# A gated mix of local attention and a GeGLU FFN: two down weights' low parts on VectorE in the second FFN, and one operand group copied two places later

## Chip, core and metric

The kernel runs on one core of one Trainium2 chip. The metric is the device time of one execution in microseconds; the median of three runs is compared. A core has five engines that work side by side, each through its own instructions in a fixed order: TensorE (PE, with PEld for loading its weights), VectorE (DVE), ScalarE (ACT), GpSimd (POOL) and SyncE (SP, which here issues most DMAs). They wait for one another through semaphores. On-chip memory is SBUF; matmul results go to PSUM, in banks of 128 x 512 floats.

## What is computed

```python
x = A_x                                                # 2048 tokens x 512
g = _sigmoid((x * gate_w).sum(-1, keepdims=True))
a = _A_ref(x, A_wqkv, A_wo)                            # 32 heads of 16; each token sees 8 tokens, 2 apart
b = (_gelu(x @ w_gate) * (x @ w_up)) @ w_down          # 512 -> 1792 -> 512
return g * a + (1 - g) * b
```

In `_A_ref` queries, keys and values come from `x @ wqkv`; each query takes a softmax over the 8 keys at distances 0, 2, ..., 14 and mixes those values; the result goes through `wo`. All inputs are float32.

## The kernel before

**Two halves.** The tokens are split into even and odd ones (`par` 0 and 1), since attention at distance 2 never mixes the two. The order is: queries, keys, values of half 0; FFN of half 0 (`ffn(0)`, here the first FFN); the same for half 1 (`ffn(1)`, the second FFN); then the last products of attention with `wo`. Attention itself (scores, softmax, mix) is VectorE work on 128 x 2048 tiles. It is written as one long generator, `attention()`, and `pull(budget)` takes about so many microseconds of it at many points of the program, so that it runs beside TensorE's products.

**Two parts of every operand.** To keep float32 precision on TensorE, every operand is split into a high part (the value rounded to the matmul's type, `float32r`) and a low part (value minus high part), and each product is three matmuls: high x high, high x low, low x high. A low part is made in one of two ways:

- on VectorE: ScalarE copies the value to the high part, then VectorE subtracts it (`tensor_tensor`, lines 725 and 762);
- by DMA: ScalarE writes the negated high part where the low part is to be, then POOL issues a DMA that adds the value to it in memory (lines 732 and 765), and ScalarE writes the high part later (lines 734 and 767).

**The FFN.** It runs over 14 chunks of 128 hidden columns (`f`, `FC = 14`). In a chunk, gate and up are computed together as one 2 x 2 block product in seven block products instead of eight (a Strassen-Winograd form: `a11`, `a12`, `s1` ... on the token side, `b11`, `t1`, ... on the weight side). `gate_up` (line 833) writes them in this order: a11 x b11, s1 x t1, the a22 x t4 of the chunk before (`fourth`), s2 x t2, a12 x b21, s4 x b22, s3 x t3. Each is six matmuls of line 774. ScalarE empties the banks (lines 779, 785, 851, 866, 882), VectorE adds (786), multiplies gate by up (790) and, after ScalarE's high part (792), makes the low part of the hidden rows (793).

Between the products there are nine **places**, `idle(0)` to `idle(8)`. At place i the steps that `ffn` registered with `at(i, ...)` are put, and a budget of attention is pulled. There are also four **pieces**: in chunks 0 and 1 of the first FFN the last projections (`project_one`), in chunks 0 and 1 of the second the last two key products (`key_one`, line 512, whose results POOL adds to memory in lines 509 and 510), and from chunk 2 on the down products of an earlier pair of chunks (`down`, line 805, matmuls in line 816). One down product takes 128 tokens through both chunks of a pair: three matmuls with the first chunk's hidden rows and down weights, three with the second's. So chunk 2's pieces, the first down products, need the down weights and the hidden rows of chunks 0 and 1.

**What a chunk prepares for the next.** In chunk f, `ffn` registers for chunk f + 1:

- `operands(par, f + 1, 0)`, the first group (t1, t2, b11), two steps. In the first FFN the first step is the ScalarE copy of line 721 and the second VectorE's subtraction of line 725; the parts are then stored in memory (`keep_parts`, at place 0 of the next chunk). In the second FFN the first step is one DMA issue on SP's queue that reads those stored parts back (line 715, 768 KB), and the second does nothing.
- `operands(par, f + 1, 1)`, the second group, made by DMA (729, 732 and 734).
- `fetch_d`, the load of raw down weights (695), and `down_w`, which splits them. Chunks 0 and 1 have theirs split together, in chunk 1, at places 3 and 7.

**What sets the order.** The text of the kernel gives the order in which instructions are traced. A planner in the compiler then orders each engine's instructions by priority (the traced order, with attention put 150 places behind by `pull`) on a timeline of its own, and assigns buffers: a tile is given a buffer of its tag when an earlier one is free (`g0`, the first groups, has two; `d`, the down weights, four). An instruction wrapped in `paced` isn't planned before the last matmul traced ahead of it. On the chip each engine goes through the planned order and waits where data isn't there.

The constants that matter: `WARM`, `BEHIND = 150`, `PACE = (0.9, 1.22)`, and `BUFS` in line 52.

Of the kernel before, what the change touches and what calls it, by code (L numbers as in the profile page):

```python
# [44 lines left out]
def tile_gated_mix(ctx: ExitStack, tc: tile.TileContext, xt, wqkv, wff, wo, out):  # L45
# [11 lines left out]
    def tl(tag, dt=F32):  # L57
        return pool.tile([P, COLS.get(tag, 512)], dt, name=tag, bufs=BUFS[tag])
# [453 lines left out]
    def key_one(k, t):  # L512

        if k == 5:
            KB[t] = bank(f"acc{t}")
        key_mm(KB[t], t, *KEYS[k], (0, 1), k == 5)
        st = tl("rt")
        nc.scalar.activation(st, KB[t], AF.Copy)
        store_b(nc.gpsimd, st, BT + t if k == 5 else t, 1, accum_op=OP.add)
        pull(1.1)  # L520
        if k == 6 and t == BT - 1:
            done.add((1, 2))

    def project_one(par, jj):

        ps = bank(f"acc{jj % BT}")
        qkv_mm(ps, par, jj, 2, range(KC))
        take(ps, par, jj, 1, tag=None if jj < 5 else "c")
        pull((2.7, 2.2)[par])
        if jj == NP - 1:  # L530
            done.add((par, 2))
# [94 lines left out]
    def paced(ins):  # L626

        tc.add_manual_dep(ins.ins, LAST[-1].ins.name, mybir.DependencyInfo(mybir.DependencyClass.Sync,
                          mybir.DependencyReason.SCHED_ONLY), reason="pace")
# [76 lines left out]
    def operands(par, f, i):  # L706


        n = len(GROUPS[i]) * QW
        w = tl(f"g{i}", F32R)  # L710
        hi, lo = w[:, :n], w[:, n:2 * n]
        for k, op in enumerate(GROUPS[i]):
            WG[f, op] = hi[:, k * QW:(k + 1) * QW], lo[:, k * QW:(k + 1) * QW]
        if par and not i:
            nc.sync.dma_start(w[:, :2 * n].bitcast(F32), WS[f, i])
            yield
            return
        raw = RAW[f][:, (0, 4)[i] * QW:][:, :n]
        if not i:
            KEEP[f] = w[:, :2 * n]  # L720
            ins = nc.scalar.activation(hi, raw, AF.Copy)
            if f:
                paced(ins)
            yield
            ins = nc.vector.tensor_tensor(lo, raw, hi.bitcast(F32), op=OP.subtract)
            if f:
                paced(ins)
            return
        ins = nc.scalar.activation(lo, raw, AF.Copy, scale=-1.0)  # L729
        if par and not f:  # L730
            paced(ins)
        nc.gpsimd.dma_start(lo.bitcast(F32), raw, accum_op=OP.add)  # L732
        yield
        ins = nc.scalar.activation(hi, raw, AF.Copy)
        if par or f:
            paced(ins)

    def keep(f):

        WS[f, 1] = dram.tile([P, 2 * QW], F32, name=f"ws{f}1")  # L740
        paced(nc.sync.dma_start(WS[f, 1], RAW[f][:, 5 * QW:7 * QW]))
# [13 lines left out]
    def down_w(par, f):  # L755
        d = WD[f] = tl("d", F32R)
        rd = RD.pop(f)
        if not par and f < 2:

            paced(nc.scalar.activation(d[:, :512], rd, AF.Copy))  # L760
            yield
            paced(nc.vector.tensor_tensor(d[:, 512:], rd, d[:, :512].bitcast(F32), op=OP.subtract))
            return
        paced(nc.scalar.activation(d[:, 512:], rd, AF.Copy, scale=-1.0))  # L764
        nc.gpsimd.dma_start(d[:, 512:].bitcast(F32), rd, accum_op=OP.add)  # L765
        yield
        paced(nc.scalar.activation(d[:, :512], rd, AF.Copy))
# [37 lines left out]
    def down(par, gr, t, b):  # L805
        if b == t == gr == 0:
            ACC.update((t, bank(f"acc{t}")) for t in range(BT))
        pp = bank("p") if b else ACC[t]
        if b and gr:
            nc.scalar.activation(pp, RT[BT + t], AF.Copy)  # L810
        ts = slice(t * P, (t + 1) * P)
        for i in range(2):
            hh_, hl_ = Hs[2 * gr + i, b]
            d = WD[2 * gr + i]
            for n, (a, w) in enumerate(((hh_, d[:, :512]), (hh_, d[:, 512:]), (hl_, d[:, :512]))):
                LAST[:] = [nc.tensor.matmul(pp, a[:, ts], w, start=(i == 0 and n == 0 and gr == 0),  # L816
                                            stop=(i == 1 and n == 2), skip_group_check=True)]
        jj = BT * b + t
        if gr == NG - 1 and par:
            nc.scalar.activation(pp, pp, AF.Copy, scale=gc[:, par, jj:jj + 1])  # L820
            ACC[jj] = pp
        elif gr == NG - 1:
            st = tl(("s", "c")[t % 2])[:, :512]
            nc.scalar.activation(st, pp, AF.Copy, scale=gc[:, par, jj:jj + 1])
            nc.gpsimd.dma_start(out_v[2 * jj], st)
        elif b:
            if gr == 0:
                RT[BT + t] = tl("rt")
            nc.scalar.activation(RT[BT + t], pp, AF.Copy)
        if par or gr < NG - 2:  # L830
            pull(1.2 * PACE[par])
# [95 lines left out]
    def ffn(par):  # L927
        XOP.update(((n, kc), X[par, blk, kc + k]) for n, blk, k in (("a11", 0, 0), ("a12", 0, 2), ("a22", 1, 2))
                   for kc in range(2))
        todo = iter(())  # L930
        for f in range(FC):
            do = {}

            def at(i, x, *args):
                do.setdefault(i, []).append(lambda: x(*args))

            if par and f < 2:
                pieces = [[lambda t=t: key_one(5 + f, t)] for t in range(BT)]
            elif f > 1:
                pieces = [[lambda b=b, i=i: down(par, f // 2 - 1, f % 2 * 2 + i, b)] for b in range(2) for i in range(2)]  # L940
            else:
                pieces = [[lambda jj=jj: project_one(par, jj) for jj in jjs]
                          for jjs in (((0, 1), (2, 3), (4, 5), (6,)), ((7,), (), (), ()))[f]]
            if f + 1 < FC:
                for i in range(2):
                    steps = operands(par, f + 1, i)
                    at(1 + 2 * i, next, steps, None)
                    at(5 + i, next, steps, None)
                at(0 if f != 1 else 5, fetch_d, f + 1)
                for g_ in ((), (0, 1))[f] if f < 2 else (f,):  # L950
                    steps = down_w(par, g_)
                    at(2 if f > 2 else 4 - f % 2, next, steps, None)
                    at(7, next, steps, None)
            else:
                steps = down_w(par, f)
                at(1, next, steps, None)
                at(4, next, steps, None)
            if par:
                if f + 2 < FC:
                    at(0, fetch_sums, f + 2)  # L960
                else:
                    at(0, fetch_o) if f + 2 == FC else None
                if f + 1 == FC:
                    todo = chain(load_o(), channels_of(0, 0))
                    for i in range(1, 9):
                        at(i, next, todo, None)
            else:
                if f + 2 < FC:
                    at(1, fetch, f + 2)
                    at(8, combine, f + 2)  # L970
                else:
                    at(0, fetch_x, 1, f + 2 - FC)
                if f + 1 < FC:
                    do.setdefault(0, []).insert(0, lambda: keep(f + 1))
                at(0, keep_parts, f)
                if f + 2 == FC:
                    at(8, early)
                if f + 1 == FC:
                    todo = before()
                    for i in range(2, 9):  # L980
                        at(i, next, todo, None)
            gate_up(par, f, pieces, do)
        for _ in todo:
            pass
        fourth()
        if par:
            out_first()
            oT = {}
        ends = iter(()) if par else tail()
        for b in range(2):  # L990
            for t in range(BT):
                down(par, NG - 1, t, b)
                if par and t == 0:
                    oT[0, b] = channels(par, 0, b)
                next(ends, None)
        if par:
            finish(oT)
# [10 lines left out]
    def load_o():  # L1008
        t = tl("g1", F32R)
        cols = [t[:, i * 512:(i + 1) * 512] for i in range(4)]  # L1010
        for u in range(NU):
            raw = WO[u]
            WO[u] = hi, lo = pair("S") if u > 1 else cols[2 * u:2 * u + 2]
            split_by_dma(hi, lo, raw)
            yield
# [213 lines left out]
```

## Time and profile before

| | us |
|---|---|
| median of three runs (606.63 to 607.61) | 606.99 |
| the profiled execution | 607.57 |
| its span, first to last instruction | 605.8 |
| PE busy in the span | 593.1 |
| DVE busy | 534.1 |
| ACT busy | 415.0 |
| POOL busy | 93.2 |

The mean granted clock of TensorE in the profiled execution is 0.994 of full speed.

How to read the rows: a row of the order of time is start, duration, engine, line, operation, output<-inputs by the names of tiles, shapes, and the number of instructions merged; in square brackets is how long the engine sat idle before it and for what. A row of the waits table is engine, line and tile that waited, what ended the wait, then total us, how often, and the longest. A row of stretches is the stretch, its length, busy time with instruction count of PE, PEld, DVE, ACT and POOL, then the granted clock, the share of DMA engines busy and GB/s. In rows of the chain of waits an entry `DMA d<-r` is the time from the issue of a DMA to its landing. SPq marks what SP's queue does.

### The profile page before, as it was taken

The page shows a single profiled execution, that of the slowest core. Times are in us where ns is not written, and L with a number is a line of the kernel's source. Part 1 is how long each engine was busy: PE and PEld are TensorE (multiplying, and loading weights), DVE is VectorE, ACT ScalarE, POOL GpSimd, SP SyncE. Part 2 cuts the span into 40 slices and gives each one's busy share as a digit, 9 for nine tenths or more (in the row PEclk, how much of TensorE's full clock was granted, in tenths as well). Part 3 has the DMA queues.
Part 4 walks back from the last instruction along what each step waited for, and adds up shares of the span by engine and source line. Part 5 has one row for each costly group of instructions (what it writes and reads, how often), then busy time and mean ns, then how long its engine had stood idle before and what let it go on. Part 6 is the DMA issues. An engine that isn't in the chain of part 4 may idle for free.

```text
span 605.8 us, 8237 instructions
## 1 busy us (share of the span) xinstructions
PE 593.1 (98%) x2767; PEld 495.8 (82%) x2767; DVE 534.1 (88%) x626; ACT 415.0 (68%) x724; POOL 93.2 (15%) x116
## 2 busy tenths in 40 slices
PE   9999989999999999999999997999999999999997
PEld 7898868888888888888899876888888888888885
DVE  6958899997999979997989993999799989998981
ACT  6663666678776787778876673766776687696622
POOL 0140000111111111112001671111111111121300
PEclk9999999999999999999999997999999999999999
DMA  8795996959786886998999999588967896967824
GB/s 281 248 265 163 288 310 200 272 159 277 193 211 210 239 239 187 246 293 254 271 273 324 268 270 289 153 215 207 259 174 184 233 253 165 240 161 200 118 63 156
DMA packets 90808, 136.47 MB, mean 225 GB/s; under 512 B 8463, under 2 KB 54671, under 8 KB 90766
## 3 DMA queue, kind: packets, MB, share of 16 engines
q1 hardware_dynamic: 70542, 102.98, 52.6%
q0 software_dynamic: 15584, 30.48, 27.4%
q10 hardware_dynamic: 4640, 2.49, 1.4%
q8 instruction: 21, 0.34, 0.2%
q14 instruction: 21, 0.17, 0.1%
HBM read 69.83 MB, written 42.56 MB: 186 GB/s over the span
## 4 chain that ended last, share of the span: by engine, by line
PE 87%; DMA 7%; ACT 1%; DVE 1%; SPq 1%; issue 1%; ACTq 0%; DVEq 0%
PE p L774 40%; PE acc L816 13%; PE p L816 13%; PE p L1046 5%; PE acc L504 5%; PE acc L406 2%; DMA d<-r 2%; PE p L355 2%; PE p L406 2%; PE acc L355 2%; PE acc L1046 2%; DMA kq<-kq 1%; DMA qs<-hl 1%; PE p L504 1%; DMA qs<-c 1%; DMA vs<-hl 1%
## 5 line engine op out<-in xcount | busy, mean ns | idle before, releaser
L774 PE MATMUL p<-S,g 128*128 128x512 f32 x672 | 168.6, 390 | 0.7 <-ACT s L779 0.7
L774 PEld LDWEIGHTS p<-S,g 128*128 128x128 f32 x672 | 126.3, 188 | 27.3 <-ACT s L779 1.1
L774 PE MATMUL p<-A,g 128*128 128x512 f32 x504 | 125.3, 389 | 1.0 <-ACT c L882 1.0
L774 PEld LDWEIGHTS p<-A,g 128*128 128x128 f32 x504 | 94.4, 188 | 20.8 <-ACT c L882 1.4
L567 DVE TENSOR_TENSOR prod<-kq 128x2048 f32<-128x2048 f32 x32 | 72.9, 2278 | 4.6 <-DMA kq<-kq 4.4
L605 DVE TENSOR_TENSOR prod<-v,lg 128x2048 f32<-128x2048 f32 x32 | 72.9, 2279 | 0.9
L570 DVE TENSOR_REDUCE lg<-prod 128x128 f32<-128x2048 f32 x32 | 73.0, 2282 | 0.2
L816 PE MATMUL p<-d,hh 128*128 128x512 f32 x224 | 68.6, 389 | 0.0
L816 PE MATMUL acc<-d,hh 128*128 128x512 f32 x224 | 60.5, 395 | 4.6 <-DMA d<-r 4.6
L732 POOL DMA_DIRECT2D g<-raw x28 | 24.3, 868 | 230.5 <-ACT g L729 133.1
L785 ACT ACTIVATE c<-p 128x512 f32<-128x512 f32 x56 | 33.4, 597 | 32.6 <-PE p L774 32.6
L816 PEld LDWEIGHTS acc<-d,hh 128*128 128x128 f32 x224 | 42.7, 191 | 13.9 <-DMA d<-r 5.0
L779 ACT ACTIVATE s<-p 128x512 f32<-128x512 f32 x56 | 33.1, 594 | 23.6 <-PE p L774 22.8
L816 PEld LDWEIGHTS p<-d,hh 128*128 128x128 f32 x224 | 42.0, 188 | 8.7
L793 DVE TENSOR_TENSOR hl<-c,hh 128x512 fp32r<-128x512 f32 x56 | 38.3, 684 | 11.2 <-ACT hh L792 11.1
L765 POOL DMA_DIRECT2D d<-r x26 | 22.3, 858 | 159.7 <-ACT d L764 133.5
L816 PE MATMUL p<-d,hl 128*128 128x512 f32 x112 | 42.6, 389 | 0.0
L786 DVE TENSOR_TENSOR c<-c,s 128x512 f32<-128x512 f32 x56 | 38.3, 684 | 3.4 <-ACT c L785 3.1
L792 ACT ACTIVATE hh<-c 128x512 fp32r<-128x512 f32 x56 | 35.1, 627 | 7.6 <-DVE c L790 7.3
L609 DVE TENSOR_TENSOR prod<-prod 128x1024 f32<-128x1024 f32 x32 | 39.0, 1219 | 0.2
L790 DVE TENSOR_TENSOR c<-c 128x512 f32<-128x512 f32 x56 | 38.2, 684 | 0.5 <-ACT c L882 0.2
L816 PE MATMUL acc<-d,hl 128*128 128x512 f32 x112 | 36.0, 395 | 0.0
(213 smaller groups left out, 993.6 us busy)
## 6 DMA issues: line engine op xcount, KB each, us to landing
g<-raw POOLq DMA_DIRECT2D x28, 512.0 KB, 7.2
raw<-wff SPq DMA_DIRECT2D x42, 256.0 KB, 3.9
ws<-g SPq DMA_DIRECT2D x14, 768.0 KB, 5.6
g<-ws SPq DMA_DIRECT2D x14, 768.0 KB, 7.6
r<-wff SPq DMA_DIRECT2D x28, 256.0 KB, 4.1
d<-r POOLq DMA_DIRECT2D x26, 256.0 KB, 6.7
v<-vs SPq DMA_DIRECT2D x8, 512.0 KB, 6.3
os<-tb SPq DMA_DIRECT2D x64, 64.0 KB, 4.7
```

Source lines behind the costliest of these rows:

```text
L504: LAST[:] = [nc.tensor.matmul(ps, x[:, ts], w, start=(start and kc == i == 0), stop=(kc == 1 and i == 2), skip_group_check=True)]
L567: paced(nc.vector.tensor_tensor(prod, spans(k, jj), q[:, jj:jj + 2, None, :].to_broadcast([P, 2, W, UC]), op=OP.mult))
L570: nc.vector.tensor_reduce(two_of(lg, jj), prod.rearrange("p j w (h d) -> p (j w) h d", d=DH), axis=AX.X, op=OP.add)
L605: paced(nc.vector.tensor_tensor(prod.rearrange("p j w (h d) -> p (j w) h d", d=DH), spans(v, jj).rearrange("p j w (h d) -> p j w h d", d=D ...
L609: nc.vector.tensor_tensor(prod[:, :, :4], prod[:, :, :4], prod[:, :, 4:], op=OP.add)
L774: LAST[:] = [nc.tensor.matmul(ps, w_, a_, start=(start and kc == 0 and n == 0), stop=(kc == 1 and n == 2), skip_group_check=True)]
L786: nc.vector.tensor_tensor(c, c, s, op=OP.add)
L790: nc.vector.tensor_tensor(ge, ge, up, op=OP.mult)
L792: nc.scalar.activation(hh_, ge, AF.Copy)
L793: nc.vector.tensor_tensor(hl_, ge, hh_.bitcast(F32), op=OP.subtract)
L816: LAST[:] = [nc.tensor.matmul(pp, a[:, ts], w, start=(i == 0 and n == 0 and gr == 0), stop=(i == 1 and n == 2), skip_group_check=True)]
L1046: LAST[:] = [nc.tensor.matmul(pa, a, b, start=(first and n == 0), stop=(last and n == 2), skip_group_check=True)]
```

## The change

```diff
@@ -755,7 +755,7 @@
     def down_w(par, f):
         d = WD[f] = tl("d", F32R)
         rd = RD.pop(f)
-        if not par and f < 2:
+        if f < 2:
 
             paced(nc.scalar.activation(d[:, :512], rd, AF.Copy))
             yield
@@ -944,7 +944,7 @@
             if f + 1 < FC:
                 for i in range(2):
                     steps = operands(par, f + 1, i)
-                    at(1 + 2 * i, next, steps, None)
+                    at(1 + 2 * (i or f == 1), next, steps, None)
                     at(5 + i, next, steps, None)
                 at(0 if f != 1 else 5, fetch_d, f + 1)
                 for g_ in ((), (0, 1))[f] if f < 2 else (f,):
```

The first edit concerns the second FFN alone (`par` = 1): the low parts of the down weights of chunks 0 and 1 are made by VectorE, as in the first FFN, and no longer by DMA. At place 3 of chunk 1 ScalarE then writes the high parts, at place 7 VectorE subtracts. Lines 764, 765 and 767 keep the other 24 down weights.

The second edit concerns chunk 1 of both FFNs: the first step for chunk 2's first group stands at place 3 instead of place 1. At place 3 it is traced ahead of the second group's first step and of the first steps of `down_w`. In all other chunks the expression gives the same places as before.

## The prediction

> **What bounds the kernel now.** I read the page first: its engine table, then the table of who waited for whom on TensorE, then the order of time around the one long wait.
>
> ```profile
> span 605.8 us, 8237 instructions
> PE 593.1 (98%) x2767; PEld 495.8 (82%) x2767; DVE 534.1 (88%) x626; ACT 415.0 (68%) x724; POOL 93.2 (15%) x116
> PE acc L816 <- DMA d<-r: 4.6, 1, 4.6
> PE p L774 <- ACT c L882: 1.0, 1, 1.0
> PE p L774 <- ACT s L779: 0.7, 1, 0.7
> ```
>
> TensorE is busy for 98% of the span, so only what makes TensorE wait, or slows its clock, can be won. One wait stands out: 4.6 us in line 816 (the down product), for a DMA that writes `d`, the down weights. It is in the second FFN. The order of time on PE:
>
> ```profile
> 359.10 2.88 PE L774 MATMUL p<-A,g 128*128 128x512 f32 x12
> 361.82 0.39 PE L816 MATMUL acc<-d,hh 128*128 128x512 f32 x1
> 366.77 0.80 PE L816 MATMUL acc<-d,hh 128*128 128x512 f32 x1 [4.56 <-DMA d<-r]
> 370.35 1.84 PE L774 MATMUL p<-S,g 128*128 128x512 f32 x6
> 372.03 0.61 PE L816 MATMUL acc<-d,hh 128*128 128x512 f32 x2
> ...
> 366.77 3.78 PE acc L816 x8
> ...
> 362.20:366.77 4.57, 0.01 (x2) 0.00 (x1) 4.18 (x5) 1.88 (x3) 2.77 (x3) 0.71 1.25 193
> 366.77:368.00 1.23, 1.23 (x3) 1.04 (x4) 0.00 (x0) 0.00 (x0) 0.00 (x0) 0.50 1.28 246
> 371.00:372.00 1.00, 1.00 (x5) 0.83 (x5) 0.00 (x0) 0.00 (x0) 0.00 (x0) 1.00 1.12 264
> 87.20:88.60 1.40, 0.73 (x2) 0.30 (x2) 1.40 (x2) 1.40 (x3) 0.21 (x1) 1.00 1.01 335
> ```
>
> The first matmul of the first down product runs at 361.82 with the high part of the weights; the second needs the low part and starts at 366.77. In the last four rows (stretches, with the granted clock third from the end) the clock is 0.50 right after the wait and 1.00 again by 371. So the wait is paid twice. At full clock a matmul starts every 2.72 / 12 = 0.227 us (359.10 to 361.82). From 366.77 to 372.03 there are 8 + 6 = 14, worth 3.17 us, and they took 5.26: **2.09 us lost to the slow clock**, beside **4.56 us of waiting**, 6.65 in all.
>
> The Trainium skill ("TensorE: Matmul & The Clock Gate", Part 1: The HAM clock gate) says that the array falls to half rate after an idle window of about 3.4 us and comes back after about as long busy. By that the slow stretch would be worth an estimated 1.7 us and the sum below 0.4 us smaller. The trace agrees on the half rate, and shows some 4 us of it.
>
> Why is the low part late?
>
> ```profile
> 353.23 1.15 ACT L764 ACTIVATE d<-r 128x512 fp32r<-128x512 f32 x2
> 354.85 0.90 POOL L765 DMA_DIRECT2D d<-r  x1 [0.27 <-ACT c L866]
> 356.51 0.86 POOL L765 DMA_DIRECT2D d<-r  x1 [0.76 <-DVE prod L567]
> DMA to landing us min/median/max: 11.6/11.7/11.9
> 359.70 1.15 ACT L767 ACTIVATE d<-r 128x512 fp32r<-128x512 f32 x2
> L762 DVE TENSOR_TENSOR d<-r,d x2: 682/682/683, 95.1 to 95.7; 128x512 fp32r<-128x512 f32 x2
> ```
>
> ScalarE writes the negated high part by 354.4, POOL issues two accumulating DMAs at 354.85 and 356.51, and each takes 11.6 to 11.9 us to land: 354.85 + 11.9 is the end of the wait. The last row is the other way, used in the first FFN for the same two chunks: one VectorE instruction of 0.68 us.
>
> **The change, part by part.**
>
> Removed: the two DMAs of line 765, and two of the four ScalarE copies of `d` (about 0.57 each by the rows above, L764 and L767). The wait for that landing goes: **-4.56**. If no pause of that length follows, the slow clock goes too: **-2.09**. That a short pause leaves the clock alone is in the last stretch above: 87.20 to 88.60 comes right behind a 1.0 us wait and has 1.00.
>
> Added: two VectorE subtractions at place 7 of chunk 1, each 0.68 us (two start 0.6 apart, 95.1 to 95.7), some 1.3 us. They need the high parts, now written at place 3 (about 354, by the L764 row), and are paced behind the product of place 7, whose end is the 359.10 at which PE goes on. What stands in VectorE's queue there:
>
> ```profile
> 359.03 2.28 DVE L567 TENSOR_TENSOR prod<-kq 128x2048 f32<-128x2048 f32 x1
> 361.23 0.68 DVE L786 TENSOR_TENSOR c<-c,s 128x512 f32<-128x512 f32 x1
> 361.83 0.68 DVE L790 TENSOR_TENSOR c<-c 128x512 f32<-128x512 f32 x1
> 362.43 2.28 DVE L570 TENSOR_REDUCE lg<-prod 128x128 f32<-128x2048 f32 x1
> 364.63 0.68 DVE L790 TENSOR_TENSOR c<-c 128x512 f32<-128x512 f32 x1
> 365.23 0.68 DVE L793 TENSOR_TENSOR hl<-c,hh 128x512 fp32r<-128x512 f32 x1
> 365.83 0.55 DVE L574 TENSOR_TENSOR lg<-lg,mask 1x392 f32<-1x392 f32 x1
> 373.38 0.69 DVE L793 TENSOR_TENSOR hl<-c,hh 128x512 fp32r<-128x512 f32 x1 [7.00 <-ACT hh L792]
> 373.99 0.68 DVE L581 TENSOR_REDUCE m<-lg 128x64 f32<-128x512 f32 x1
> 363.46 0.62 ACT L792 ACTIVATE hh<-c 128x512 fp32r<-128x512 f32 x1
> ```
>
> Program order puts the subtractions behind L786 and the first L790, and ahead of attention (L567, L570). Either they go before L567 (359.03 to 360.3, both parts early), or behind the first L790 (362.43 to 363.7). The down product needs the first at 362.05 and the second three matmuls later, 362.7: a wait of nothing, or about 1 us. If one of them waits, attention and chunk 1's hidden rows (L790, L793) stand behind it. As cover VectorE has 7.00 us of idle at 366.4, which exist because PE stood; they go with the stall.
>
> **What is late next** is in the same rows. The down product of one block runs over both chunks, and chunk 1's hidden rows are ready only at 363.46 + 0.62 = 364.1 (high) and 365.23 + 0.68 = 365.9 (low), where an unhindered PE wants them at 362.5 and 362.95. The stall on the weights covered this. Left in place, that is a rest of up to 3 us, the subtractions ahead of it another 1.2. But the planner draws the order anew: in the first FFN, with VectorE making these parts, TensorE's only waits are the two short ones in the waits table (1.0 and 0.7), both before chunk 2's down products. I take a rest of **+1.4**, the low half of 0 to 4.2, because two ScalarE copies fewer (1.15 us, right ahead of L792) and a product that needs none of this (370.35, line 774, 1.36 at full clock) can fill part of it.
>
> Moved: the first step of chunk 2's first group, from place 1 to 3 of chunk 1, in both FFNs. In the second it is one SP transfer of 768 KB:
>
> ```profile
> SPq L715 <- PE p L774: 44.7, 10, 7.1
> 341.99 0.47 SPq L715 DMA_DIRECT2D g<-ws  x1
> 352.72 0.34 SPq L715 DMA_DIRECT2D g<-ws  x1
> g<-ws SPq DMA_DIRECT2D x14, 768.0 KB, 7.6
> ```
>
> Ten of fourteen issues waited for a product to free the buffer, and chunk 3's, which stands in chunk 2's program, went out at 352.72, while PE was still in chunk 1. So program place hardly sets the issue; I take 0. At worst chunk 2's goes out with chunk 3's at 352.72, lands 7.6 later at 360.3, and the product at 359.10 waits 1.2.
>
> In the first FFN the step is one ScalarE copy, paced behind the product before its place; it issues no DMA, and VectorE's half of it stays at place 5:
>
> ```profile
> 83.51 0.85 ACT L721 ACTIVATE g<-raw 128x768 fp32r<-128x768 f32 x1 [4.81 <-DVE raw L701]
> 85.26 1.28 ACT L882 ACT_TABLE_LOAD   x1 [0.42 <-DMA qs<-c]
> 87.05 1.05 ACT L729 ACTIVATE g<-raw 128x1024 fp32r<-128x1024 f32 x1
> ```
>
> ScalarE stands 4.81 us at L721 until VectorE has combined the weights; later, that wait is gone. But the 1.0 us wait of PE hangs on L882, which the DMA of `qs` holds until 85.2, so it stays; the 0.7 us wait hangs on L779, behind L729, and the moved copy (0.85) joins just that queue. Between -0.7 and +0.85: I take 0.
>
> At the end of the span VectorE is needed once more:
>
> ```profile
> 594.36 0.69 DVE L87 TENSOR_TENSOR hl<-raw,hh 128x512 fp32r<-128x512 f32 x1 [6.60 <-ACT hh L86]
> 595.75 0.62 PE L1046 MATMUL p<-S,hh 128*128 128x512 f32 x2
> ```
>
> The last attention rows are split by 595.05, and the last products that can need them start at 595.75: 0.7 us to spare at least. VectorE falls back by at most 1.3 against PE, so 0 to 0.6; its later gaps take some of it. I take 0.
>
> Sum: -4.56 - 2.09 + 1.4 + 0 + 0 = **-5.25 us**. The profiled execution took 607.57 (605.8 of span and 1.8 around it), so 602.3. It stands 0.58 above the median of the runs shown, 606.99, so I forecast **601.7 us** for the median.
>
> **The rivals.**
>
> 1. *The hidden rows take the stall's place.* Queues stay as they are, with the weights on time. PE waits for the rows from 362.5 to 364.1 and to 365.9, or 367.1 with the subtractions ahead. That block's last matmul, the fifth of the eight behind the stall, started near 366.77 + 4 x 0.45 = 368.6; it would start at 365.9 to 367.1, so 1.5 to 2.7 earlier. The nine behind it that still ran slowly (369.0 to 372.03, for 9 x 0.227 = 2.04) give 1.0 more. Gain 2.5 to 3.7: **603.3 to 604.5**. For it: the rows above. Against it: the planner knows VectorE's times and can put other products first.
> 2. *Slower: VectorE's queue becomes the wait.* If the subtractions are put behind the scores (L574 ends at 366.38) and two softmax steps like L581 (0.68), the second ends at 366.4 + 1.3 + 1.3 = 369.0, 2.2 later than the landing, and the longer pause keeps the slow clock. It decides when the second subtraction ends after 366.77. It gives **607.3 to 609.2**. Against it: attention stands behind everything else by rule, and has to here.
> 3. *The change doesn't do what it says.* Something else holds the product at 359.10 or 361.82 to about the same time, for instance the transfer of chunk 2's group, issued late and landing at the slowest rate of the two DMAs above (11.9 after 352.72 is 364.6), with the slow clock behind it: a gain of 0 to 2, **605.0 to 607.0**.
>
> **How the numbers follow.** Forecast 0.55, with 599.5 (all 6.65 won and half of the two short waits) to 602.9 as its own range; rival 1 0.25; rival 2 0.12; rival 3 0.08. From 599.5 to 605.8 lie forecast, rival 1 and part of rival 3, about 0.82. A measurement of this kernel tells 0.2%, 1.2 us, from no change. Faster by more: 0.55 + 0.25 + 0.02 = 0.82; within: 0.06; slower by more: 0.12.
>
> **What would show it.** Right: no wait of PE for a DMA at line 816, the granted clock 1.00 from 350 to 385, line 765 at 24 instructions, 762 at 4, and VectorE's 7 us gap gone. The rest term: any wait of PE near the first down product of the second FFN for L792 or L793. The move: chunk 2's issue in line 715 still near 342, and the two short waits near 87 within 1 us in sum. Wrong: a new wait of PE elsewhere over 2 us, or the subtractions of line 762 ending after 362.7 with PE waiting for them.

## The result and the profile after

| | before | after |
|---|---|---|
| median, in us (5 runs each) | 606.63 (606.30 to 607.61) | 602.34 (601.03 to 604.45) |
| ratio to before, 95% interval | | 0.9932 [0.9907, 0.9958] |
| the profiled execution | 607.57 | 604.45 |
| its span | 605.8 | 601.9 |
| its mean granted clock | 0.994 | 0.996 |

The change makes the kernel faster by 0.7%; 601.7 was forecast. The profiled execution of the changed kernel happens to be the slowest of the five: its span is 3.9 us shorter than before's, and the five spans run from 599.3 to 601.9. Its trace holds a stretch near 90 us at half clock that a second trace of the same kernel, below, doesn't have.

The page of the changed kernel (its last row: a kind of DMA, how many, the size of one, the median us from issue to landing), and below it TensorE's waits (line, what ended the wait, total us, count, longest):

```profile
span 601.9 us, 8224 instructions
PE 592.3 (98%) x2767; PEld 495.5 (82%) x2767; DVE 535.4 (89%) x628; ACT 414.1 (69%) x722; POOL 91.5 (15%) x114
d<-r POOLq DMA_DIRECT2D x24, 256.0 KB, 6.7
```

```profile
PE p L774 <- ACT s L779: 2.2, 1, 2.2
PE acc L816 <- DMA d<-r: 0.4, 1, 0.4
```

The 4.6 us for `d` are gone; 0.4 are left, and two waits of 1.0 and 0.7 us have become one of 2.2.

**Where the time came from: the second FFN.** TensorE's order of time in the changed kernel, then VectorE's, then stretches with the granted clock third from the end:

```profile
360.54 1.52 PE L774 MATMUL p<-A,g 128*128 128x512 f32 x6
361.90 0.84 PE L816 MATMUL acc<-d,hh 128*128 128x512 f32 x3
362.58 1.52 PE L774 MATMUL p<-A,g 128*128 128x512 f32 x6
363.94 0.39 PE L816 MATMUL acc<-d,hh 128*128 128x512 f32 x1
...
382.42 1.20 PE L816 MATMUL acc<-d,hh 128*128 128x512 f32 x4 [0.41 <-DMA d<-r]
```

```profile
359.86 0.68 DVE L786 TENSOR_TENSOR c<-c,s 128x512 f32<-128x512 f32 x1
360.52 1.29 DVE L762 TENSOR_TENSOR d<-r,d 128x512 fp32r<-128x512 f32 x2
361.73 2.29 DVE L567 TENSOR_TENSOR prod<-kq 128x2048 f32<-128x2048 f32 x1
...
367.93 0.68 DVE L793 TENSOR_TENSOR hl<-c,hh 128x512 fp32r<-128x512 f32 x1
...
369.60 0.69 DVE L793 TENSOR_TENSOR hl<-c,hh 128x512 fp32r<-128x512 f32 x1 [0.52 <-ACT hh L792]
```

```profile
362.00:364.00 2.00, 2.00 (x11) 1.65 (x10) 2.00 (x2) 0.58 (x1) 1.96 (x2) 1.00 1.14 202
364.00:366.00 2.00, 2.00 (x11) 1.65 (x10) 2.00 (x4) 1.82 (x3) 0.49 (x2) 1.00 1.44 183
```

The two subtractions (line 762, x2, 1.29 us) run ahead of attention's L567 and end at 361.81, before the first down product starts at 361.90. TensorE goes on without a pause, at clock 1.00, where before it stood 4.56 us and then ran slowly. VectorE's gap of 7.00 us has shrunk to 0.52. Chunk 1's hidden rows are no earlier for it: the low part of the first 512 tokens, which the first down products need, ends at 368.6, where before it ended at 365.9 (that of the other 512 ends at 370.3, before at 374.1). Yet nobody waits: the new planned order puts matmuls with the first chunk's rows first, and between and behind them products that need none of this (362.58 and the next).

**Where time was given back: the first FFN.** TensorE's order of time, ScalarE's, and the stretches:

```profile
84.42 1.52 PE L774 MATMUL p<-A,g 128*128 128x512 f32 x6
88.10 4.54 PE L774 MATMUL p<-S,g 128*128 128x512 f32 x12 [2.15 <-ACT s L779]
92.48 0.62 PE L774 MATMUL p<-A,g 128*128 128x512 f32 x2
```

```profile
84.72 1.28 ACT L882 ACT_TABLE_LOAD   x1 [3.58 <-DMA qs<-c]
...
87.46 0.59 ACT L779 ACTIVATE s<-p 128x512 f32<-128x512 f32 x1
...
88.93 0.86 ACT L721 ACTIVATE g<-raw 128x768 fp32r<-128x768 f32 x1
```

```profile
88.00:90.00 2.00, 1.90 (x5) 1.52 (x6) 1.88 (x4) 2.00 (x5) 0.70 (x1) 0.50 0.49 100
90.00:92.00 2.00, 2.00 (x7) 1.59 (x6) 1.97 (x4) 2.00 (x5) 0.00 (x0) 0.65 0.87 168
```

Before, two matmuls of chunk 2's first product (a11 x b11) stood between the two waits. That product needs the group whose copy (L721) was moved. With the copy at 88.93, seven ScalarE instructions later in the planned order, the planner puts these two matmuls behind s4 and s3 (92.48, 12 matmuls later). Nothing is left to fill the pause, it grows to 2.15 us, and here the clock falls to 0.50 at its end (for 3.41 us, 87.97 to 91.38): 12 matmuls take 4.54 us, where 3.01 is their time at full clock (the rows of edit 1 alone, below, which also show the two matmuls in their old place). The length of the pause alone doesn't decide whether the clock falls, as the experiments show.

For the same work, from chunk 0's a22 x t4 to the matmul of line 774 behind the first four of line 816 (below: the stage), TensorE took 11.78 us before (80.64 to 92.42) and 13.52 after (80.34 to 93.86).

**And at the end.** TensorE's last row and the last issue on SP's queue, first in the changed kernel, then in the kernel before:

```profile
595.62 1.07 PE L1046 MATMUL p<-S,hl 128*128 128x512 f32 x4
```

```profile
598.08 0.39 SPq L1093 DMA_DIRECT2D out<-rt  x1
```

```profile
600.96 0.39 PE L1046 MATMUL p<-S,hl 128*128 128x512 f32 x1
```

```profile
602.01 0.33 SPq L1093 DMA_DIRECT2D out<-rt  x1
```

The new planned order ends with four low parts in one go, where before it ended with one, so the last results come free together and ScalarE empties three of the four banks one after another (596.05 to 597.64). The last store is issued 1.39 us behind TensorE's end (598.08 - 596.69); before it was 0.66 (602.01 - 601.35).

**The sum.** The second FFN's first product started at 326.95 before and at 328.39 after:

```profile
326.95 1.54 PE L774 MATMUL p<-A,g 128*128 128x512 f32 x6
```

```profile
328.39 1.54 PE L774 MATMUL p<-A,g 128*128 128x512 f32 x6
```

So 1.44 us were lost up to there. From there to TensorE's end it took 274.40 us before (to 601.35) and 268.30 after (to 596.69): 6.10 less, that is the forecast 6.65, less 0.41 for the wait at 382.42, and 0.14 that no row names. The tail grew by 0.75 (4.45 to 5.2). 1.44 - 6.10 + 0.75 = -3.9, the difference of the spans. What lies around the span differed too, 1.8 before and 2.5 after, which no row explains.

### The profile page after: what moved, and what is told of

Same layout as the page of the kernel before. It is cut to its first block, busy times and chain, and to the rows that moved or that the text cites. A ratio compares the mean times of both kernels' runs of the same rounds, so it can differ in the third digit from the quotient of the medians.

```text
span 601.9 us, 8224 instructions
## 1 busy us (share of the span) xinstructions
PE 592.3 (98%) x2767; PEld 495.5 (82%) x2767; DVE 535.4 (89%) x628; ACT 414.1 (69%) x722; POOL 91.5 (15%) x114
## 4 chain that ended last, share of the span: by engine, by line
PE 86%; DMA 9%; ACT 1%; issue 1%; DVE 1%; SPq 1%; ACTq 0%; DVEq 0%; POOLq 0%
PE p L774 41%; PE p L816 12%; PE acc L816 12%; PE acc L504 5%; PE p L1046 5%; PE acc L406 2%; PE p L406 2%; PE acc L1046 2%; PE acc L355 2%; PE p L355 2%; DMA r<-wff 1%; DMA d<-r 1%; DMA ks<-hh 1%; DMA kq<-kq 1%; DMA vs<-hh 1%
## 5 line engine op out<-in xcount | busy, mean ns | idle before, releaser
L774 PE MATMUL p<-S,g 128*128 128x512 f32 x672 | 170.7, 392 | 2.2 <-ACT s L779 2.2
L567 DVE TENSOR_TENSOR prod<-kq 128x2048 f32<-128x2048 f32 x32 | 72.9, 2278 | 4.0 <-DMA kq<-kq 4.0
L793 DVE TENSOR_TENSOR hl<-c,hh 128x512 fp32r<-128x512 f32 x56 | 38.4, 686 | 7.0 <-ACT hh L792 6.9
L765 POOL DMA_DIRECT2D d<-r x24 | 20.5, 856 | 152.6 <-ACT d L764 124.8
L779 ACT ACTIVATE s<-p 128x512 f32<-128x512 f32 x56 | 33.1, 595 | 14.9 <-PE p L774 14.4
L790 DVE TENSOR_TENSOR c<-c 128x512 f32<-128x512 f32 x56 | 38.3, 684 | 1.7 <-ACT c L882 1.6
L792 ACT ACTIVATE hh<-c 128x512 fp32r<-128x512 f32 x56 | 35.1, 627 | 3.5 <-DVE c L790 3.4
L829 ACT ACTIVATE rt<-p 128x512 f32<-128x512 f32 x48 | 28.3, 595 | 9.8 <-PE p L816 9.6
```

What stands on the lines that cost most here:

```text
L567: paced(nc.vector.tensor_tensor(prod, spans(k, jj), q[:, jj:jj + 2, None, :].to_broadcast([P, 2, W, UC]), op=OP.mult))
L774: LAST[:] = [nc.tensor.matmul(ps, w_, a_, start=(start and kc == 0 and n == 0), stop=(kc == 1 and n == 2), skip_group_check=True)]
L790: nc.vector.tensor_tensor(ge, ge, up, op=OP.mult)
L792: nc.scalar.activation(hh_, ge, AF.Copy)
L793: nc.vector.tensor_tensor(hl_, ge, hh_.bitcast(F32), op=OP.subtract)
```

## The experiments

Three things were to be told apart: which of the two edits does what; why TensorE stands near 87 us, and what the move does to it; and why a low part made by DMA is so late at that place, because two such DMAs slow each other or because of other traffic. All times are medians in us; each ratio is to runs of the kernel before on the same chip.

**Edit 1 alone** (the first hunk of the diff, without the second).

> Edit 1 alone (the two down weights' low parts on VectorE in the second FFN); chunk 2's first group stays at place 1. Theory A (edit 1 brings the whole gain and the move costs): the first FFN is as before, with its two short waits of TensorE near 87 us (1.0 and 0.7) and the clock at 1.00 there; the stall of 4.6 us is gone; 5.0 to 5.9 us faster than before, 600.7 to 601.6, and so 0.5 to 2 faster than the changed kernel. Theory B (the move has a share in the gain, through the 4.8 us that ScalarE no longer waits): 603 to 604.5.

601.48 (600.17 to 602.09) against 607.31; ratio 0.9902 [0.9879, 0.9925]. TensorE near 87 us:

```profile
86.28 0.73 PE L774 MATMUL p<-A,g 128*128 128x512 f32 x2 [0.31 <-ACT c L882]
87.72 3.01 PE L774 MATMUL p<-S,g 128*128 128x512 f32 x12 [0.70 <-ACT s L779]
```

The two matmuls stand between the waits, as before, and the clock stays at 1.00. The stage takes 11.10 us (80.37 to 91.47). The whole gain is here without the move. The second FFN, from its first product to TensorE's end, takes 268.32 us, against 268.30 with both edits and 274.40 before. That edit 1 alone should also be 0.5 to 2 faster than both edits is weighed further down, on one chip.

**Edit 2 alone** (the second hunk, without the first).

> Edit 2 alone (the move to place 3), the down weights as before. Theory A: TensorE waits once for 2.2 us near 86 us and the clock falls to half behind it; the 4.6 us stall in the second FFN stays; 0.2 to 1.9 us slower than before, 606.8 to 608.5. Theory B: 604.5 to 606.2, faster than before.

608.74 (606.54 to 613.69) against 607.31; ratio 1.0028 [1.0003, 1.0053]. The old stall is there, and a slow stretch behind it (six matmuls in 2.71 us):

```profile
86.07 3.01 PE L774 MATMUL p<-S,g 128*128 128x512 f32 x12 [1.04 <-ACT s L779]
...
364.41 0.80 PE L816 MATMUL acc<-d,hh 128*128 128x512 f32 x1 [3.83 <-DMA d<-r]
...
367.99 2.71 PE L774 MATMUL p<-S,g 128*128 128x512 f32 x6
```

The move gains nothing alone. In this execution the DMA of `qs` had landed earlier (82.6), the pause near 87 was 1.04 us and the clock stayed at 1.00. So theory A's pause of 2.2 us and the half clock aren't in this trace, and its stage (10.85 us) doesn't account for the slower median, which lies 0.24 above theory A's range. The execution traced (606.77) is the second fastest of the twelve. The three longest (610.57 to 613.69) have the lowest mean clock, 0.989 and 0.990 against 0.993 in the trace; where in them it fell isn't recorded.

**Both edits, without the DMA behind L882.** A table load of ScalarE (L882) waits for a buffer that the DMA of `qs` reads. Here the block's stage takes a buffer of another tag, and the order of every engine's instructions is that of the changed kernel:

```diff
-        take(ps, par, jj, 1, tag=None if jj < 5 else "c")
+        take(ps, par, jj, 1, tag=None if jj < 5 else "s" if jj == 5 else "c")
```

> The changed kernel, but the projection of token block 5 is staged in an s buffer instead of a c buffer, so that the gelu of line 882 finds a free c buffer and waits for no DMA. The order on every engine is that of the changed kernel. Theory A (the 2.2 us wait of TensorE near 86 hangs on this DMA, by way of line 882 and line 779 behind it on ScalarE): line 882 runs near 82, line 779 before 86, the wait is gone and with it the half clock; 598.6 to 600.5. Rival (the wait hangs on the second group's copy of line 729, planned ahead of line 779, or on something behind it): a wait of 1 to 2 us stays, 601 to 602.5.

601.46 (599.59 to 605.68) against 607.31; ratio 0.9916 [0.9887, 0.9945]. ScalarE, then TensorE:

```profile
83.11 1.28 ACT L882 ACT_TABLE_LOAD   x1
...
89.11 0.63 ACT L792 ACTIVATE hh<-c 128x512 fp32r<-128x512 f32 x1 [1.72 <-DVE c L790]
89.64 0.58 ACT L779 ACTIVATE s<-p 128x512 f32<-128x512 f32 x1
```

```profile
87.73 1.52 PE L774 MATMUL p<-S,g 128*128 128x512 f32 x6
90.27 1.65 PE L774 MATMUL p<-S,g 128*128 128x512 f32 x6 [1.02 <-ACT s L779]
```

L882 no longer waits, and the 2.15 us pause is gone: the DMA of `qs` was its cause. But the median is the rival's (601 to 602.5) and not theory A's (598.6 to 600.5), and so is the wait that stays, for something behind line 729. A new pause of 1.02 us comes in the middle of the twelve: the second L779 stands behind L792, which now waits 1.72 us for VectorE. The stage takes 10.83 us (82.29 to 93.12), 2.7 less than in the changed kernel's first trace. Its span (602.1) is no shorter all the same: an earlier wait, in line 355 for L86, was 1.8 us in this execution and 0.5 in the other, and at its end the clock fell to 0.50, from 8.0 to 11.4 us.

**Edit 1 and the same buffer.**

> Edit 1 alone with the same other buffer for block 5. Theory A: line 721, back at place 1, holds ScalarE until 83.5 for VectorE, so line 882 still comes at about 85 and little is won: 0 to 0.6 us faster than edit 1 alone, 600.2 to 601.5, and 0.5 to 2 slower than the changed kernel with this buffer. So the move pays only where this DMA isn't in the way. Rival (the DMA alone made the waits): both waits near 87 go, 1.5 to 2 faster than edit 1 alone, 599 to 600.

601.47 (599.97 to 603.50) against 607.31; ratio 0.9913 [0.9888, 0.9937]. The wait for L882 is gone, the 0.7 us for L779 stays, the stage takes 10.90 us (81.02 to 91.92). Against edit 1 alone the time doesn't move: in that kernel this wait had been 0.31 us. The second half of theory A missed: this kernel was to be 0.5 to 2 slower than both edits with the same buffer, and the medians are 601.47 and 601.46. So the move doesn't pay with the DMA out of the way either.

**The changed kernel again, and edit 1 alone again,** on another chip, whose kernel before took 608.03 (604.13 to 610.64).

> The changed kernel once more, on one chip with edit 1 alone, to weigh the move by itself. Edit 1 alone and the changed kernel differ by one ScalarE copy and two matmuls of chunk 2 that stand 12 matmuls later. Theory A (the move costs): 0.5 to 2 us slower than edit 1 alone. Theory C (the move does nothing on the whole: the wait near 86 lasts as long as the DMA of the projection's stage takes, whichever way): within 0.5 of edit 1 alone. Either way 4 to 6 faster than before.

> Edit 1 alone once more. Theory A: 0.5 to 2 us faster than the changed kernel of the same call. Theory C: within 0.5 of it.

Both edits: 603.24 (599.76 to 605.84), ratio 0.9927 [0.9905, 0.9948]. Edit 1 alone: 602.93 (600.79 to 606.40), ratio 0.9923 [0.9897, 0.9948]. They can't be told apart. The trace of both edits, TensorE and the stretch:

```profile
87.28 3.02 PE L774 MATMUL p<-S,g 128*128 128x512 f32 x12 [2.14 <-ACT s L779]
```

```profile
87.00:89.00 2.00, 1.72 (x7) 1.42 (x8) 1.88 (x3) 2.00 (x5) 0.85 (x1) 1.00 0.36 75
```

The same pause, 2.14 us, and this time the clock stays at 1.00: the twelve matmuls take 3.02 us and not 4.54. The stage takes 11.96 us, and 10.81 in the trace of edit 1 alone. Part of that difference is only the DMA of `qs`, which lands at another time in each execution. From the start of L882's table load to the end of the stage, the two traces with the move and full clock (this one and that of edit 2 alone) take 7.59 us, and the six with the old place, the same buffer and full clock 7.12 to 7.17. So behind L882 the move costs 0.45 us, the two matmuls that no longer fill the pause. L882 itself starts 3.3 to 4.4 us into the stage with the move and 3.4 to 4.6 us without it, which doesn't tell the two apart.

A fall of the clock costs some 1.55 us more (9.14 in the first trace of both edits). The granted clock of every execution is on record: it is 0.996 or less, as in that trace, in 5 of 17 executions with both edits and in 1 of 20 with edit 1 alone. That is too few to tell the rates apart, and where the clock fell in the others isn't recorded.

**One weight each.** VectorE makes only chunk 0's low part, or only chunk 1's; the other is made by DMA, alone in its place:

```diff
-        if not par and f < 2:
+        if f < (1 if par else 2):
```

```diff
-        if not par and f < 2:
+        if f < 2 and (not par or f == 1):
```

> VectorE makes only chunk 0's low part; chunk 1's still comes by one accumulating DMA. Theory Q (a DMA there lands 11 to 12 us after its issue because of the key products' accumulating DMAs in the same queue): with the issue near 355 it lands near 366 to 367, TensorE waits for it at line 816 or the planner puts other products first; a part of the stall stays, 602.5 to 605. Rival P (the two weights' DMAs slow each other down, alone one lands in about 7): it lands near 362, no stall at line 816, 601 to 602.5.

> VectorE makes only chunk 1's low part; chunk 0's, which the down product needs first, comes by one accumulating DMA issued near 355. Theory Q: it lands near 366 and TensorE stalls at line 816 for about 4 us with the clock at half behind it, so nearly nothing is won: 605 to 607.5. Rival P: it lands near 362, the stall is under 1 us, 601 to 603.

Chunk 0's alone: 604.75 (601.93 to 606.41) against 608.03, ratio 0.9949 [0.9928, 0.9969]. POOL's issue of chunk 1's DMA, how long the DMAs of line 765 took to land, and TensorE's one wait in line 816:

```profile
355.95 0.90 POOL L765 DMA_DIRECT2D d<-r  x1
```

```profile
DMA to landing us min/median/max: 3.2/6.4/11.8
```

```profile
383.37 1.20 PE L816 MATMUL acc<-d,hh 128*128 128x512 f32 x4 [1.51 <-DMA d<-r]
```

Chunk 1's alone: 606.78 (604.56 to 608.86) against 608.03, ratio 0.9989 [0.9965, 1.0012]. The same three views:

```profile
353.94 1.36 POOL L765 DMA_DIRECT2D d<-r  x1
```

```profile
DMA to landing us min/median/max: 3.2/6.4/12.7
```

```profile
366.65 0.79 PE L816 MATMUL acc<-d,hh 128*128 128x512 f32 x1 [4.65 <-DMA d<-r]
```

A DMA alone in that place takes 11.8 or 12.7 us, no less than the 11.6 to 11.9 of the pair. So the two didn't slow each other. What does delay `d` stays open. Around it in POOL's queue stand the accumulating DMAs of the key products (lines 509 and 510), as theory Q says, and no run took them away. But SP's queue is slow there too: in the kernel before, of the transfers issued from 345 to 365 us, those of 64 KB took 9.4 us to land, where the median of all 64 is 4.7:

```profile
os<-tb SPq DMA_DIRECT2D x4, 64.0 KB, 9.4
```

So load on all DMA engines, whichever the queue, is a rival that no run tested. Which low part is on VectorE matters: with chunk 1's, the stall is whole (4.65 us: 353.94 + 12.7 = 366.6), since the first down product needs chunk 0's first. With chunk 0's, the planner fills the time until chunk 1's has landed (367.8), and TensorE runs from 360 to 380 without a pause at clock 1.00. Its second FFN takes 269.41 us to TensorE's end, so 4.99 of the 6.10 us are won; chunk 1's alone takes 275.14.

The trace of chunk 0's alone shows one thing more, in the first FFN, where every engine's order is that of edit 1 alone. The copy of L721 isn't moved, the two matmuls stand in the pause, and the clock falls all the same:

```profile
86.85 0.73 PE L774 MATMUL p<-A,g 128*128 128x512 f32 x2 [0.80 <-ACT c L882]
88.28 4.61 PE L774 MATMUL p<-S,g 128*128 128x512 f32 x12 [0.70 <-ACT s L779]
```

```profile
89.00:92.00 3.00, 3.00 (x9) 2.33 (x8) 2.97 (x6) 2.95 (x6) 0.00 (x0) 0.50 0.88 173
```

Two pauses of 0.80 and 0.70 us were enough here, so the half clock of the first trace isn't the move's doing alone. It also makes this trace longer: its stage takes 13.19 us, 2.38 more than in edit 1 alone on this chip, and that has nothing to do with the weight.

**Three weights.** The wait at 382.42 is for chunk 2's own down weights, by DMA. Edit 1 carried on to them, without the move, and edit 1 alone beside it:

```diff
-        if not par and f < 2:
+        if f < (3 if par else 2):
```

> Edit 1 carried on: in the second FFN VectorE makes the low part of chunk 2's down weights too (condition f < (3 if par else 2)); the move of chunk 2's first group is left out, as in the kernel with edit 1 alone, and the subtraction stands at place 3 or 7 of chunk 2's own program. The theory that any down weight whose DMA is issued here lands too late says that the wait of 0.4 to 0.8 us in line 816 near 380, which all kernels with edit 1 keep, goes, and that nothing takes its place: 0.4 to 0.9 us less than edit 1 alone, 600.6 to 602.5 if the kernel before takes 607 to 608, line 765 at 23 instructions. The rival says that the subtraction stands in VectorE's queue ahead of hidden rows that are wanted at once, so that a wait for L793 or L790 of about the same size replaces it: no difference from edit 1 alone.

> Edit 1 alone once more, on the same chip as the kernel with three weights, to compare the two. 0.8% to 1.0% faster than the kernel before, with a wait of 0.4 to 0.8 us in line 816 near 380 for a DMA that writes d.

601.53 (599.67 to 604.17), ratio 0.9901 [0.9867, 0.9936], against 601.50 (599.77 to 603.09), ratio 0.9900 [0.9870, 0.9930], for edit 1 alone; the kernel before took 607.35. In the trace the three parts are there (line, count, min/median/max ns, starts):

```profile
L762 DVE TENSOR_TENSOR d<-r,d x5: 683/685/693, 93.5 to 373.0; 128x512 fp32r<-128x512 f32 x5
```

TensorE has no wait in line 816 any more (0.7 us in edit 1 alone), and no wait for L790 or L793 has come in its place. The medians are equal all the same; the two spans are 598.9 and 598.7, and the one with three weights holds an earlier wait of 1.3 us in line 355 for L86, a wait that changes from execution to execution. From the second FFN's first product to TensorE's end the two traces take 268.02 and 268.61, so the 0.6 us are there; in the medians a gain of this size can't be seen. No version tried beats edit 1 alone by more than this spread.

## Why the prediction was right, and where it was not

- **The stall (-4.56) and the slow clock behind it (-2.09)** went as worked out. In the trace the second FFN gained 6.10 of the 6.65, and where the stall stays (4.65 us with chunk 1's part alone) the time stays too. The second FFN takes 268.2 to 268.7 us to TensorE's end in all seven traces in which VectorE makes just these two parts, and 274.4 to 275.1 in the three with the stall. Rival 3 falls with this.
- **The two subtractions** took the first of the two ways described, ahead of attention, and end at 361.81. Rival 2 needed an end after 366.77; it is refuted by 5 us.
- **The rest (+1.4)** was mis-sized. At that place it is 0. The hidden rows come just when rival 1 said, with the subtractions ahead of them: 368.6, less the 1.44 us by which this FFN starts later, is 367.2, and rival 1 has 367.1. But the planned order changed so that nobody needs them then. The prediction had named this, but as filling only part of the gap. What came in its place is smaller and lies elsewhere: 0.41 us (0.4 to 0.8 in the other traces of both edits or edit 1 alone, 0.7 and 0.2 with the other buffer) for chunk 2's weights, which their DMA brings late now that TensorE comes sooner. The run with three weights confirms whose wait it is.
- **The end of the span (0, range 0 to 0.6)** cost 0.75. The reason given, VectorE late with the last rows, isn't what happened; the planned order of the last products changed. TensorE's end to the span's end is 5.2 to 5.3 in every kernel in which VectorE makes any of these parts, 4.45 before and 4.6 with the move alone.
- **The move (0)** had the wrong mechanism for the first FFN; that its cost, 0.45 us, lies "between -0.7 and +0.85" is luck. For the second FFN it was right: there chunk 2's transfer was issued 1.87 us later than before, of which 1.44 is the later start of the whole FFN, and the next one 1.44 later. Counted from that start, chunk 2's issue comes after 15.5 us here and 15.6 to 16.5 in the other traces with the move, 15.0 to 19.2 in those without, so its place in the program doesn't set it:

```profile
343.86 0.50 SPq L715 DMA_DIRECT2D g<-ws  x1
354.16 0.34 SPq L715 DMA_DIRECT2D g<-ws  x1
```

  For the first FFN the step counted the copy's time in ScalarE's queue and rightly kept the wait on the DMA of `qs`, as the run with the other buffer shows. It didn't ask what the copy feeds: two matmuls that filled the pause went with it. The sign named for a wrong prediction, a new wait over 2 us elsewhere, did appear (2.15), and in this execution the clock fell at its end. What the runs show in place of the 0 is 0.45 us, those two matmuls. Over all runs this is small: both edits against edit 1 alone give 0.9927 and 0.9923 on one chip, and the move alone 1.0028 [1.0003, 1.0053]. Whether the move makes the clock fall more often stays open, since it fell without the move too; so does the slower median of the move alone.
- **That a short pause leaves the clock alone** was read from one stretch of one trace. It held where the stall had been (clock 1.00 there in every trace without the stall), but it is no rule: behind 0.80 and 0.70 us near 87 the clock fell in the trace of chunk 0's part alone.

That the forecast of 601.7 is only 0.6 us from the median is partly luck, because errors of both signs cancel: -1.4 for the rest, +0.41 for chunk 2's weights, +0.75 for the end, and +1.44 in the traced execution from the first half.

On the clock, the Trainium skill ("TensorE: Matmul & The Clock Gate", Part 1) puts the fall behind an idle window of about 3.4 us and says that this window runs freely. The traces agree on the step: every stretch of half clock behind a pause lasts 3.41 or 6.83 us. They differ on the length of the pause: 2.15 us were enough once, and 0.80 and 0.70 another time. That 2.14 us were not enough in another execution fits a window whose start the kernel doesn't set; how much of a window must be idle, these runs don't settle.

## What to carry to other kernels

A step that is moved takes its consumers along: look not only at what it queues with, but at which products it makes possible, and whether one of them is filling somebody's pause. When a stall goes and a planner draws the order anew, don't price the next late item by the old order; here time came back at places for which the old trace shows no wait, a transfer 20 us later and the tail. And where two transfers are late, ask which is needed first: making that one another way carried most of the gain here, and making only the other one gained nothing that could be measured.

## What the hardware showed

- A pause of TensorE of 2.15 us ended in 3.41 us at clock 0.50 (87.97 to 91.38), and one of 2.14 us at the same place, in another execution, in none. Two pauses of 0.80 and 0.70 us there ended in 3.41 us at 0.50 once (88.89 to 92.30); in the other traces with pauses of up to 1.04 us there the clock stayed at 1.00.
- In the stall of the kernel before, the clock fell 1.96 us after TensorE stopped (at 364.17) and stayed at 0.50 for 6.82 us, to 370.99; of these TensorE worked 4.2.
- An accumulating DMA of 256 KB took 11.8 and 12.7 us to land between POOL's key-product DMAs, alone as well as in a pair, and a median of 6.7 over the 24 in the changed kernel. The Trainium skill ("DMA: Bandwidth & Descriptors", Anatomy of one DMA) gives a fit of 2.0 us and 436 KB per us more, an estimated 2.6 us for this size; these runs show a multiple of it.
- Executions of one and the same kernel differ more than the first three runs let expect: 604.13 to 610.64 for the kernel before on one chip.
